# A delta-rule attention and two MLP layers in one kernel: layer 1 regrouped into six blocks of four chunks, with a longer opening chain

## The chip, the cores and the metric

The kernel runs on one core of a Trainium2 chip. TensorE (PE) multiplies matrices, VectorE (DVE), ScalarE (ACT) and GpSimd (POOL) work elementwise, SyncE (SP) issues the DMAs; each has its own instruction stream and waits for others by semaphores. The metric is the device time of one execution in microseconds (us); a change of under 0.5% can't be told from none here.

## The reference

```
attention, 4 batches x 8 heads x 768 steps, head size 48:
  k_n = k / (norm(k) + 1e-6);  state = 0
  per step t:  y[t]  = q[t] @ state
               state = state + beta[t] * outer(k_n[t], v[t] - k_n[t] @ state)
layer 1 (3072 tokens, 384 -> 2048 -> 384):
  h = x @ w_in
  g = h where h >= 1;  0 where h <= -1;  (h+1)^2/4 between
  x = g @ w_out
layer 2 (same sizes):  h = x @ w_in;  g = max(h, 0)^2;  out = g @ w_out
```

All data are float32. The kernel splits each operand of a layer into a rounded high part and a low remainder and sums three products (high x high, low x high, high x low).

## The kernel before

**Chunks, groups, blocks.** The 768 steps are 24 chunks of 32 steps, 128 tokens each (four batches). Attention works chunk by chunk: a gram of keys and queries (`gram`, L293), and a triangular inversion per group of chunks (`tri`: DVE transposes, a chain of small multiply-adds in `step`, on DVE for group 0, on POOL for the others). A chunk's chain is then `ks` (keys times state, L484), `tr` (inverse times values, L498), `qs` and `pu` (the two parts of y, tile yy, L484 and L518), `ku` (state update, tile sps, L530) and `xt` (transposes of y, L559). Each of these is 32 float32 matmuls of 32 rows, which the trace shows as 64 (two passes). `GROUPS` and `SIZES` say how many chunks make an inversion group and a layer-1 block.

**The opening** (all before `SL = 2 * NF`) is written out by hand: group 0 is two chunks, whose inverse is made of two halves on DVE and joined by small products (`joined`: ld writes z, L449; dld writes w, L457). Four more grams, for group 1, are made there too. The state update of these two chunks (`ku`) stands later, beside units 2 and 3.

**Units.** A unit is one of 16 slices of a layer's 2048 columns for one block: nine matmuls into h (L574, `hidden`), the activation on ACT and DVE, and nine matmuls into acc (`out1`) two units later. Layer 1's matmuls are as wide as the block, 256 or 384 columns; layer 2 uses 512. `exa` and `exb` hang the later chunks' steps, inversions and loads on half-unit slots; PE's order is as written, the others' is set by a scheduler after the opening.

**Weights.** Layer 1's 32 tiles come as 64-bit words (L160, at most two loads under way) and are joined, tile by tile, by two ACT passes (L178, L181), one DVE pass (L187), then split by ACT (L198) and DVE (L202), 128x384 each. Layer 2's go through DRAM and are placed during the last block.

Of the kernel before, what the change touches and what calls it, by code (L numbers as in the profile page):

```python
# [19 lines left out]
SIZES = [2, 2, 3, 3, 3, 3, 3, 2, 3]  # L20

GROUPS = [2, 4, 4, 4, 4, 4, 2]
# [3 lines left out]
def kernel(  # L26
# [39 lines left out]
    EAGER = 18  # L66
    AHEAD = 8
    RG = 3
    RAW = 3
    KQ, KG = 4, 2  # L70
    WT, WL = 3, 4
    GB = 2
    MANY = 4
    HEAD = 19
# [14 lines left out]
    pairs = {}  # L89

    def weight(i, f):

        if (i, f) not in pairs:
            t = wp.tile([P, 2, DM], F32R, tag=f"w{i}{f}", name=f"w{i}{f}")
            pairs[i, f] = t[:, 0], t[:, 1]
        return pairs[i, f]
# [4 lines left out]
    early = ["att0", "acc0", "att1", "acc1", "acc2"]  # L101
# [16 lines left out]

    def load_kq(c):
        if c < NCH:  # L120
            kqt[c] = fetch_kq(c, "kqt", KQ)

# [3 lines left out]
    def load_kg(c):  # L126
        if c < NCH and c not in kqg:
            kqg[c] = fetch_kq(c, "kqg", KG)

    def fetch_kq(c, tag, bufs):  # L130
        t = ring.tile([P, B2, H, 2 * T], F32, tag=tag, bufs=bufs, name="kqt")
        for o in range(2):
            nc.sync.dma_start(
                t[64 * o:64 * o + D].rearrange("p b h x -> p (b h x)"), kq[c, D * o:D * (o + 1)]
            )
        return t

    def load_kv(c):
        if c >= NCH:
            return  # L140
        t = kvt[c] = ring.tile([P, 2, H, D], F32, tag="kv", bufs=3, name="kv")
        nc.sync.dma_start(t.rearrange("p x h d -> p (x h d)"), kv[c])

# [5 lines left out]

    def load_w(x, key):
        w, f, i = key
        pool, tag, bufs = ring, "raw", RAW
        if w == 0:
            pool, tag, bufs = wp, f"w{i}{f}", 1
        raw = raws[key] = pool.tile([P, DM, 2], I32, tag=tag, bufs=bufs, name="raw")
# [11 lines left out]


    def convert_stages(key, box):
        def s0():
            raw = raws.pop(key)
            t = box["w"] = tmp("wt", WT)
            b = box["t"] = tmp("wl", WL)
            nc.scalar.activation(  # L178
                t, raw[:, :, 1].bitcast(F32), AF.Prelu, scale=2.0 ** -112, alpha=2.0 ** 32
            )  # L180
            nc.scalar.activation(  # L181
                b.bitcast(I32), raw[:, :, 0].bitcast(U32), AF.Copy, scale=7.49 * 2.0 ** -32
            )

        def s1():
            t, bits = box["w"].bitcast(I32), box["t"].bitcast(I32)
            nc.vector.scalar_tensor_tensor(  # L187
                bits, t, 3, bits, ALU.logical_shift_left, ALU.bitwise_or
            )

        return [s0, s1]


    def part_stages(key, box):
        _, f, i = key

        def s3():
            nc.scalar.copy(weight(i, f)[0], box["t"])  # L198

        def s4():  # L200
            hi, lo = weight(i, f)
            nc.vector.tensor_sub(lo, box["t"], hi.bitcast(F32))  # L202

        return convert_stages(key, box) + [s3, s4]
# [3 lines left out]
    def weight_items(w):  # L208

        keys = [(w, f, i) for f in range(NF) for i in range(2)]  # L210
        if w == 0:
            keys.sort(key=lambda k: (k[1] + LAG * k[2], -k[2]))

        def item(x):
            _, f, i = keys[x]
            box = {}
            if w == 0:
                r = part_stages(keys[x], box)
            else:
                r = convert_stages(keys[x], box)  # L220
                r.append(lambda: nc.sync.dma_start(w2f[f, :, i], box["t"]))
            s1 = r[1]
            r[1] = lambda: (s1(), ahead(x + 1 + (RAW if w else AHEAD)))
            return r

# [3 lines left out]
        def ahead(end):  # L229
            while todo and todo[0][0] < end:  # L230
                load_w(*todo.pop(0))
# [5 lines left out]
    def fetch_w2(f):  # L237
        w2r[f] = ring.tile([P, 2, DM], F32, tag="raw", bufs=RAW, name="w2r")
# [27 lines left out]
    def value(c):  # L266

        g, j = group_of[c]
        nc.gpsimd.tensor_mul(
# [10 lines left out]
    def gram(c, lo=0, hi=2, late=0, eng=None, side=0):  # L280
# [8 lines left out]
        src = kqt[c] if c < KQ else kqg[c]  # L289
# [9 lines left out]
        if c >= KQ:  # L299
            kqg.pop(c)  # L300
            if late < 2:
                load_kg(c + KG)
# [19 lines left out]
    HEADS = SIZES[0]  # L322
    cross = {}

    spare = {
        name: f"w{i}{NF - f}" for name, i, f in
        (("u0", 1, 1), ("u1", 1, 2), ("cross", 0, 1), ("z", 1, 3), ("l", 0, 2), ("d", 1, 4))
    }

    def cross_gram(a, c):  # L330
        x = cross[a, c] = wp.tile([P, H, 2, T], F32, tag=spare["cross"], name="cross")
# [14 lines left out]
    def tri(n, eng, halves=False):  # L346
        x = tx
        gm = ring.tile([P, T, T], F32, tag="gm", bufs=1, name="gm")
# [36 lines left out]
        def row():  # L385
            if halves:
                d = two(gm, both, both)
                eng.tensor_mul(
# [6 lines left out]
        def row2():  # L395
            if halves:
                eng.tensor_mul(
# [10 lines left out]
        def step(j):  # L408
# [15 lines left out]
            eng.tensor_add(rest, rest, t)  # L424
# [11 lines left out]
    def joined(n):  # L436
        l, z = (wp.tile([P, 2, H, T], F32, tag=spare[k], name=k) for k in "lz")
        d = wp.tile([P, GC * H, T2], F32, tag=spare["d"], name="d")
# [30 lines left out]
    def chunk_steps(c):  # L469
        n, j = block_of[c]  # L470
        g, gj = group_of[c]
        t = {}

# [22 lines left out]
        def tr():  # L496
# [7 lines left out]
            else:  # L504
                us[c] = wp.tile([P, H, D], F32, tag=spare[f"u{c}"], name="u")
            nc.scalar.copy(us[c], o)

        def qs():
            o = t["o"] = att([P, H, D], "yy", 1)
            of_state(o, 1)  # L510
            if c >= HEADS:
                kqt.pop(c)
                load_kq(c + KQ)

        def pu():
            o = t["o"]
            y = t["y"] = t["r"]
# [7 lines left out]
        def ku():  # L525
            k_ = kvt[c]
            if c < NCH - 1:
# [6 lines left out]
                if c >= HEADS:  # L534
                    pu()
# [5 lines left out]
            if c >= HEADS:  # L541
                nc.scalar.copy(t["y"], t["o"])
            done()

        def done():

            t["n"] = t.get("n", 0) + 1
            if t["n"] == 2:
                del kvt[c]
                load_kv(c + 3)  # L550

        def xt():
            if j == 0:
# [11 lines left out]
        return [ks, tr, qs, pu, ku, xt] if c < HEADS else [lambda: (ks(), qs()), tr, ku, xt]  # L565
# [18 lines left out]
    def hidden(layer, n, f):  # L584
# [18 lines left out]
        if layer == 0:  # L603
# [3 lines left out]
            marks[1] = nc.vector.tensor_scalar(g, r, 2.0, 0.5, ALU.min, ALU.mult)  # L607
            nc.scalar.activation(g, g, AF.Square)  # L608
            nc.vector.scalar_tensor_tensor(g, r, -1.0, g, ALU.add, ALU.max)  # L609
        else:  # L610
# [3 lines left out]
        def rest():  # L614
# [6 lines left out]
            nc.scalar.copy(ghi, g)  # L621
            nc.vector.tensor_sub(glo, g, ghi.bitcast(F32))  # L622
            gs[layer, n, f] = (ghi, glo)
# [8 lines left out]
    def out1(n, f):  # L632
# [10 lines left out]
        if f == NF - 1:  # L643
            for m, o in enumerate(acc.pop(n)):
                evac(m, o, x2[:, m, P * FIRST[n]:P * FIRST[n] + w], "wl", WL)
# [38 lines left out]
    def split_x2(n):  # L684
        def s0():
            homes = (("kqt", KQ), ("kqt", KQ), ("kqg", KG))
            both = [ring.tile([P, 2, N], F32R, tag=t, bufs=b, name="x2s") for t, b in homes]
            xh[n], xl[n] = ([x[:, i] for x in both] for i in range(2))
            for kt, x in enumerate(xh[n]):
# [8 lines left out]
    def flow(items, lag=1):  # L698

        steps = []  # L700
        for x, it in enumerate(items):
            for i, st_ in enumerate(it):
                while len(steps) <= x * lag + i:
                    steps.append([])
                steps[x * lag + i].append(st_)
        return [lambda fs=fs: [f() for f in fs] for fs in steps]

# [7 lines left out]
    first1, w1s = weight_items(0)  # L715
    first2, w2s = weight_items(1)
    w1f = flow(w1s)
    w1f.reverse()

    SPREAD = 3  # L720
    behind = [nullcontext]

    def more_w1(m=1):
        with behind[0]():
            for _ in range(m):
                if w1f:
                    w1f.pop()()

    with tc.manual_schedule():
        for c in range(GROUPS[0]):  # L730
            load_kq(c)
        nc.sync.dma_start(bet, beta)
        for c in range(GROUPS[0], KQ):
            load_kq(c)
        for c in range(KG):
            load_kg(KQ + c)
        for c in range(HEADS):
            load_kv(c)
        first1(EAGER)
        nc.gpsimd.memset(zero, 0.0)  # L740
        nc.gpsimd.memset(one, 1.0)
        nc.gpsimd.memset(tiny, 1e-36)
        nc.scalar.activation(st[:, 0, 0, 0:1], one, AF.Sqrt, bias=zero)
        nc.gpsimd.memset(mask, 1.0)
        nc.gpsimd.memset(tx, 0.0)
        for b in range(B):
            for o, op in enumerate((ALU.is_ge, ALU.is_gt)):
                m_ = mask[T * b:T * (b + 1), o]
                nc.gpsimd.affine_select(
# [5 lines left out]
        for c in range(GROUPS[0]):  # L755
            gram(c, 0, 1)
        begin, pre, steps, end = tri(0, V, True)
        begin()
        go(pre)
        for c in range(HEADS):  # L760
            save0(c)
        go([gram(c, late=2, eng=G) for c in range(GFIRST[1], GFIRST[2])])
        cross_gram(0, 1)
        masks = [gram(c, 1, 2, late=2, eng=G) for c in range(HEADS)]
        go(steps)
        for c in range(HEADS):
            value(c)
        go(masks)
        end()
        rows0()  # L770
        begin, pre, steps, end1 = tri(1, G)
        begin()
        ins = go(pre[:-2])
        behind[0] = lambda: tc.issue_after(ins.ins)
    ENGINES = {mybir.EngineType.PE}
    with tc.manual_schedule(engines=ENGINES):
        for f in (ld0, dld0):
            for c in range(HEADS):
                f(c)
        go(pre[-2:])  # L780
        go(steps)
        chains = [chunk_steps(c) for c in range(HEADS)]
        (k0, t0, q0, p0, _, x0), (k1, t1_, q1, p1, _, x1) = chains
# [176 lines left out]
```

## Time and profile before

| | |
|---|---|
| three runs, median (lowest to highest) | 1024.24 us (1022.86 to 1027.52) |
| the profiled execution | 1026.46 us, span of its instructions 1024.7 us |
| PE busy | 968.4 us, 95% of the span |
| DVE, ACT, POOL busy | 574.5, 465.2, 319.4 us |
| DMA | 80.83 MB, mean 79 GB/s |

A timeline row has start, length, engine, source line, operation, tiles written and read, shape, count, and in brackets the idle time of the engine before it with what ended that. "issue" as the ender means that the engine waited for nothing that the profile shows.

### The profile page before, as it was taken

Reading aid. Unit: us, or ns where it says so; the run is one execution under the profiler, and the core shown is the slowest. Engines: PE = TensorE matmul, PEld = TensorE weight load, DVE = VectorE, ACT = ScalarE, POOL = GpSimd, SP = SyncE. Lnnn points to the kernel's source line nnn. Section 1 sums busy time; section 2 is a strip of 40 time slices with the busy share of each in tenths; the row PEclk is TensorE's granted clock in tenths of the full one; section 3 lists DMA queues with packets and bytes.
Section 4 is the critical chain, followed back from the end, with each engine's and each line's share of the span. In section 5 each row is a group of like instructions: output and inputs, shape, how many; then the busy total and the mean of one; then the engine's idle time right before and its main releaser. Section 6 shows DMA issues by size and latency. Waiting matters only on the chain.

```text
span 1024.7 us, 32087 instructions
## 1 busy us (share of the span) xinstructions
PE 968.4 (95%) x14152; PEld 902.6 (88%) x14152; DVE 574.5 (56%) x994; ACT 465.2 (45%) x935; POOL 319.4 (31%) x476
## 2 busy tenths in 40 slices
PE   5357899999999999999999999999999999999998
PEld 4347898999999999999999999989989999899997
DVE  6988565775666677677465676543343333333333
ACT  2776465554555545555445554333333333333332
POOL 3792780492077049368022121120020200200000
PEclk9999999999999999999999999999999999999999
DMA  9774154442532534312023223010010000000000
GB/s 265 222 215 142 49 152 133 129 142 61 174 101 80 157 88 133 111 39 96 3 71 90 67 79 95 6 55 8 1 62 1 1 32 1 31 1 1 31 1 31
DMA packets 35244, 80.83 MB, mean 79 GB/s; under 512 B 4512, under 2 KB 15264, under 8 KB 35104
## 3 DMA queue, kind: packets, MB, share of 16 engines
q1 hardware_dynamic: 35104, 78.78, 25.9%
q8 instruction: 111, 1.82, 0.8%
q14 instruction: 29, 0.24, 0.1%
HBM read 63.03 MB, written 15.73 MB: 77 GB/s over the span
## 4 chain that ended last, share of the span: by engine, by line
PE 87%; DMA 6%; DVE 3%; ACT 2%; issue 1%; SPq 0%; ACTq 0%; DVEq 0%
PE acc L574 39%; PE h L574 38%; DMA raw<-in_w_dram 5%; PE yy L518 2%; PE sps L530 2%; PE tr L498 2%; PE ks L484 2%; PE g L293 1%; PE yy L484 1%; PE xt L559 1%; DMA kqt<-in_kq_dram 1%; DVE wl L187 0%; DVE g L609 0%; DVE w L202 0%; DVE gp L427 0%
## 5 line engine op out<-in xcount | busy, mean ns | idle before, releaser
L574 PE MATMUL acc<-w,gg 128*128 128x384 f32 x1152 | 218.4, 337 | 2.1 <-ACT e L629 2.1
L574 PEld LDWEIGHTS acc<-w,gg 128*128 128x128 f32 x1152 | 204.5, 187 | 10.7 <-ACT e L629 3.0
L574 PE MATMUL h<-x2s,w 128*128 128x512 f32 x864 | 213.8, 392 | 0.0
L574 PEld LDWEIGHTS h<-x2s,w 128*128 128x128 f32 x864 | 160.9, 188 | 28.3
L574 PE MATMUL h<-xh,w 128*128 128x384 f32 (+1 forms) x864 | 164.6, 327 | 3.5 <-ACT r L606 2.8
L574 PE MATMUL acc<-gh,w 128*128 128x384 f32 (+1 forms) x864 | 163.7, 325 | 1.6 <-ACT gh L621 1.6
L612 DVE TENSOR_TENSOR rg<-rg 128x512 f32<-128x512 f32 x96 | 71.3, 743 | 141.4 <-ACT rg L611 141.4
L574 PEld LDWEIGHTS h<-xh,w 128*128 128x128 f32 x864 | 139.6, 193 | 6.7 <-ACT r L606 3.7
L574 PEld LDWEIGHTS acc<-gh,w 128*128 128x128 f32 x864 | 136.7, 189 | 5.2 <-ACT gh L621 1.7
L611 ACT ACTIVATE rg<-h,zero 128x512 f32<-128x512 f32 x96 | 66.0, 687 | 137.4 <-PE h L574 137.4
L622 DVE TENSOR_TENSOR gg<-rg,gg 128x512 fp32r<-128x512 f32 x96 | 66.7, 695 | 104.5 <-ACT gg L621 104.5
L622 DVE TENSOR_TENSOR gl<-g,gh 128x384 fp32r<-128x384 f32 (+1 forms) x144 | 88.0, 611 | 64.5 <-ACT gh L621 60.3
L423 POOL TENSOR_TENSOR t<-tx,gm 128x30 f32<-128x30 f32 (+9 forms) x180 | 110.0, 611 | 19.3 <-DVE tx L402 5.9
L621 ACT CAST gh<-g 128x384 fp32r<-128x384 f32 (+1 forms) x144 | 68.7, 477 | 102.7 <-DVE g L609 78.4
L606 ACT ACTIVATE r<-h,one 128x384 f32<-128x384 f32 (+1 forms) x144 | 78.3, 543 | 81.5 <-PE h L574 80.3
L424 POOL TENSOR_TENSOR tx<-tx,t 128x30 f32<-128x30 f32 (+9 forms) x180 | 110.6, 615 | 14.0
L621 ACT CAST gg<-rg 128x512 fp32r<-128x512 f32 x96 | 59.7, 622 | 119.7 <-PE acc L574 112.7
L609 DVE SCALAR_TENSOR_TENSOR g<-r,g 128x384 f32<-128x384 f32 (+1 forms) x144 | 88.5, 614 | 39.9 <-ACT g L608 37.4
L607 DVE TENSOR_SCALAR g<-r 128x384 f32<-128x384 f32 (+1 forms) x144 | 62.4, 434 | 68.1 <-ACT r L606 67.1
L608 ACT ACTIVATE g<-g 128x384 f32<-128x384 f32 (+1 forms) x144 | 70.2, 487 | 54.5 <-DVE g L607 53.7
L574 PE MATMUL acc<-gl,w 128*128 128x384 f32 (+1 forms) x432 | 90.8, 318 | 1.9 <-DVE gl L622 1.9
L574 PE MATMUL h<-xl,w 128*128 128x384 f32 (+1 forms) x432 | 91.8, 322 | 0.0
(99 smaller groups left out, 923.9 us busy)
## 6 DMA issues: line engine op xcount, KB each, us to landing
raw<-in_w_dram SPq DMA_DIRECT2D x64, 384.0 KB, 3.8
kqt<-in_kq_dram SPq DMA_DIRECT2D x88, 192.0 KB, 4.1
kv<-in_kv_dram SPq DMA_DIRECT2D x24, 384.0 KB, 3.6
w2f<-wl SPq DMA_DIRECT2D x32, 192.0 KB, 3.1
w2r<-w2f SPq DMA_DIRECT2D x16, 384.0 KB, 3.0
x2r<-x SPq DMA_DIRECT2D x6, 768.0 KB, 4.8
out_dram<-e SPq DMA_DIRECT2D x23, 192.0 KB, 2.0
x<-e SPq DMA_DIRECT2D x18, 192.0 KB, 2.1
```

What stands on the lines that cost most here:

```text
L423: eng.tensor_mul(t, by.to_broadcast(shape), of.to_broadcast(shape))
L424: eng.tensor_add(rest, rest, t)
L484: per_bh(lambda b, h, p, pd: nc.tensor.matmul(o[p, h], kqt[c][pd, b // 2, h, x * T:(x + 1) * T], st[pd, b // 2, h], start=h == 0, stop=x = ...
L574: nc.tensor.matmul(o, *((r, l) if swap else (l, r)), **flags)
L606: marks[0] = nc.scalar.activation(r, h, AF.Relu, bias=one)
L607: marks[1] = nc.vector.tensor_scalar(g, r, 2.0, 0.5, ALU.min, ALU.mult)
L608: nc.scalar.activation(g, g, AF.Square)
L609: nc.vector.scalar_tensor_tensor(g, r, -1.0, g, ALU.add, ALU.max)
L611: marks[0] = nc.scalar.activation(r, h, AF.Relu, bias=zero)
L612: marks[1] = nc.vector.tensor_mul(g, r, r)
L621: nc.scalar.copy(ghi, g)
L622: nc.vector.tensor_sub(glo, g, ghi.bitcast(F32))
```

## The change

`SIZES` and `GROUPS` become six fours: every layer-1 block is one inversion group of four chunks, 512 columns wide. The opening now carries four chunks instead of two, and its order is given step by step; the full chain of the four chunks, state updates too, stands before the first unit. Grams of the first four chunks make both halves at once (`gram_of_head`), and POOL waits with its first multiplication until group 0's inversion has ended. Layer-1 weights are joined and split two tiles a pass (128x768, in place), four pairs in the opening, the rest one pair a unit inside the first twelve units (`between`). Scratch tiles share the space of the last three pairs, whose six loads come after the opening.

```diff
-SIZES = [2, 2, 3, 3, 3, 3, 3, 2, 3]
-GROUPS = [2, 4, 4, 4, 4, 4, 2]
+SIZES = [4] * 6
+GROUPS = [4] * 6
...
+    def sign_bits(raw):
+        low, high = raw[..., 0], raw[..., 1].bitcast(F32)
+        return (
+            lambda: nc.scalar.activation(high, high, AF.Prelu, scale=2.0 ** -112, alpha=2.0 ** 32),
+            lambda: nc.scalar.activation(
+                low, low.bitcast(U32), AF.Copy, scale=7.49 * 2.0 ** -32),
+        )
...
+    def upper(x):
+        nc.scalar.copy(weights(x)[:, :, 0], words[x])
+
+    def lower(x):
+        t = weights(x)
+        nc.vector.tensor_sub(t[:, :, 1], words.pop(x), t[:, :, 0].bitcast(F32))
...
+    def gram_of_head(c):
...
+        per_bh(lambda b, h, p, pd: nc.tensor.matmul(
+            g[p, h].rearrange("p x i -> p (x i)"),
+            kqt[c][pd, b // 2, h, 0:T], kqt[c][pd, b // 2, h],
+            start=h == 0, stop=True, skip_group_check=True,
+        ))
...
+    def between(f):
+        a = READY + f if READY + f < NP else None
+
+        def part(x):
+            if x == 0:
+                if a is not None:
+                    make(a)
+                some(1)
+            elif x == 1:
+                if a is not None:
+                    upper(a)
+            elif x == 2:
+                some(1)
+            elif a is not None:
+                lower(a)
...
-        chains = [chunk_steps(c) for c in range(HEADS)]
-        (k0, t0, q0, p0, _, x0), (k1, t1_, q1, p1, _, x1) = chains
-        for m, fs in enumerate([[k0, t0], [k1], [q0, p0], [t1_], [q1], [x0], [p1], [x1]]):
-            go(fs)
-            if m < 4:
-                more_w1(5)
...
+        whole_bits(2)
+        q1()
+        t2()
+        go(pre1[-2:])
+        steps1[0]()
+        go(steps1[1:])
+        whole_bits(3)
+        q2()
+        make(2)
+        k2()
+        p2()
+        upper(2)
+        y2()
+        lower(2)
+        s3()
+        dld0(3)
...
+        for x in range(NF):
+            unit(x, between(x))
```

On PE, between the last gram of the opening and the first unit, there stood in the kernel before (a group of 32 instructions a chunk and step; h is the first unit):

```order
L449 MATMUL z<-d,l 32x16 x64
L457 MATMUL w<-gp,z 32x16 x64
L498 MATMUL tr<-kv,gp 32x48 x32
L478 MATMUL ks<-u,cross 32x48 x32
L518 MATMUL yy<-u,gp 32x48 x32
L498 MATMUL tr<-kv,gp 32x48 x32
L478 MATMUL yy<-u,cross 32x48 x32
L559 MATMUL xt<-ident,kv 128x128 x3
L518 MATMUL yy<-u,gp 32x48 x32
L559 MATMUL xt<-ident,kv 128x128 x3
L574 MATMUL h<-xh,w_839 128x256 x6
```

The same stretch begins, in the changed kernel, as follows (L495, L503, L545, L525 and L531, L568 are its lines for z, w, tr, the two forms of ks and yy, and pu; 64 instructions into sps stand where the dots are):

```order
L495 MATMUL z<-room 32x16 x64
L503 MATMUL w<-gp,room 32x16 x64
L545 MATMUL tr<-kv,gp 32x48 x32
L495 MATMUL z<-room 32x16 x32
L525 MATMUL ks<-room 32x48 x32
L495 MATMUL z<-room 32x16 x32
L545 MATMUL tr<-kv,gp 32x48 x32
...
L503 MATMUL w<-gp,room 32x16 x32
L531 MATMUL ks<-st,kqt 32x48 x32
L525 MATMUL yy<-room 32x48 x32
L545 MATMUL tr<-kv,gp 32x48 x32
L531 MATMUL yy<-st,kqt 32x48 x32
```

The stretch has grown from 10 groups of 32 instructions to 26: z 4, w 4, tr 4, ks 3, yy 7 and sps 4. Nine groups of grams stand ahead of it in both.

On DVE, beside the units of the first block, there stood (wl and w are weights, g and gl the activation):

```order
L607 TENSOR_SCALAR g<-r 128x256
L202 TENSOR_TENSOR w_1252<-wl,w_1252 128x384
L202 TENSOR_TENSOR w_1262<-wl,w_1262 128x384
L187 SCALAR_TENSOR_TENSOR wl<-wt,wl 128x384
L202 TENSOR_TENSOR w_1364<-wl,w_1364 128x384
L609 SCALAR_TENSOR_TENSOR g<-r,g 128x256
```

and there stands now, once a unit:

```order
L660 TENSOR_SCALAR g<-r 128x512
L192 SCALAR_TENSOR_TENSOR wl<-raw 128x768
L663 SCALAR_TENSOR_TENSOR g<-r,g 128x512
L678 TENSOR_TENSOR gl<-g,gh 128x512
L226 TENSOR_TENSOR w_1658<-wl,w_1658 128x2x384
```

The weights, which a scheduler had laid in wherever DVE was free, now stand at fixed places between the steps of the activation, two instructions a unit.

## Rows read from the trace of the kernel before

**Rows 1.** The page's counts: PE, the instruction queue (packets, MB, share), weight loads.
```profile
PE 968.4 (95%) x14152; PEld 902.6 (88%) x14152; DVE 574.5 (56%) x994; ACT 465.2 (45%) x935; POOL 319.4 (31%) x476
...
q8 instruction: 111, 1.82, 0.8%
...
raw<-in_w_dram SPq DMA_DIRECT2D x64, 384.0 KB, 3.8
```

**Rows 2.** Busy time by stretch: its us, each engine, granted clock, DMA share, GB/s.
```profile
51.20:76.90 25.70, 14.42 (x353) 12.76 (x353) 21.81 (x29) 20.43 (x47) 23.27 (x31) 1.00 0.74 216
...
260.00:400.00 140.00, 140.00 (x2998) 132.45 (x2989) 93.58 (x167) 73.37 (x154) 66.36 (x105) 1.00 0.40 116
```

**Rows 3.** Timeline of PE in the opening.
```profile
28.30 1.54 PE L293 MATMUL g<-kqt 48*32 48x32 f32 x97 [2.67 <-issue]
29.77 0.61 PE L449 MATMUL z<-d,l 32*32 32x16 f32 x30
33.55 1.51 PE L449 MATMUL z<-d,l 32*32 32x16 f32 x98 [3.17 <-issue]
...
38.10 1.52 PE L457 MATMUL w<-gp,z 32*32 32x16 f32 x98 [2.65 <-issue]
...
43.26 1.00 PE L498 MATMUL tr<-kv,gp 32*32 32x48 f32 x34 [2.92 <-issue]
46.15 1.50 PE L478 MATMUL ks<-u,cross 32*32 32x48 f32 x64 [1.89 <-ACT u L506]
...
60.51 1.50 PE L518 MATMUL yy<-u,gp 32*32 32x48 f32 x64 [4.48 <-ACT u L506]
66.12 0.90 PE L559 MATMUL xt<-ident,kv 128*128 128x128 f32 x3 [4.11 <-ACT kv L523]
67.59 1.65 PE L574 MATMUL h<-xh,w 128*128 128x256 f32 x6 [0.57 <-ACT xh L561]
```

**Rows 4.** Timeline of PE: units of 256, 384 and 512 columns, two grams.
```profile
145.89 0.84 PE L574 MATMUL h<-xh,w 128*128 128x256 f32 x6
...
146.91 0.84 PE L574 MATMUL acc<-gh,w 128*128 128x256 f32 x6
...
163.94 1.99 PE L293 MATMUL g<-kqt 48*32 48x64 f32 x128
...
308.51 1.20 PE L574 MATMUL h<-xh,w 128*128 128x384 f32 x6
...
310.07 1.20 PE L574 MATMUL acc<-gh,w 128*128 128x384 f32 x6
...
705.39 2.21 PE L574 MATMUL h<-x2s,w 128*128 128x512 f32 x9
707.44 2.26 PE L574 MATMUL acc<-w,gg 128*128 128x384 f32 x12
```

**Rows 5.** Timeline of PE: one chunk's chain among 384-wide units.
```profile
301.21 0.88 PE L484 MATMUL ks<-st,kqt 48*32 48x48 f32 x64
...
302.70 1.32 PE L574 MATMUL acc<-gh,w 128*128 128x384 f32 x6
...
306.04 0.88 PE L498 MATMUL tr<-kv,gp 32*32 32x48 f32 x64
...
311.73 0.93 PE L530 MATMUL sps<-kv 32*48 32x48 f32 x64
...
313.40 1.31 PE L574 MATMUL h<-xh,w 128*128 128x384 f32 x6
```

**Rows 6.** Timeline of DVE: one weight pass, at two times.
```profile
36.97 0.55 DVE L202 TENSOR_TENSOR w<-wl,w 128x384 fp32r<-128x384 f32 x1
...
69.37 0.95 DVE L202 TENSOR_TENSOR w<-wl,w 128x384 fp32r<-128x384 f32 x1
```

**Rows 7.** Timeline of POOL: first and last instruction of group 1's inversion.
```profile
33.40 1.27 POOL L393 TENSOR_TENSOR gm<-gm,st 128x256 f32<-128x256 f32 x1 [0.19 <-DVE st L382]
...
82.17 0.27 POOL L424 TENSOR_TENSOR tx<-tx,t 128x30 f32<-128x30 f32 x1
```

More of the change, by code (lines that the diff above doesn't have):

```diff
@@ L185, in s1 @@
+            for f in sign_bits(raw):
+                f()
         def s1():
[L186 to L189, printed above, removed]
+            box["t"] = joined_words(box.pop("raw"), [P, DM])
         return [s0, s1]
[L194 to L204, printed above, removed]
+    words = {}
@@ L533, in ku @@
                 ))
-                if c >= HEADS:
+                if not apart:
                     pu()
@@ L582, with hidden @@
     marks = [None, None, None]
-    def hidden(layer, n, f):
+    def hidden(layer, n, f, between=lambda x: None):
         w = P * SIZES[n] if layer == 0 else N
@@ L714 @@
     V, G = nc.vector, nc.gpsimd
[L715 to L718, printed above, removed]
+    first2, w2s = weight_items()
+    SL = 2 * NF
     SPREAD = 3
[L721 to L727, printed above, removed]
+    NW, NP = 2 * NF, NF
+    EARLY, READY, HELD = 5, 4, 6
+    exa, exb = {}, {}
+    bits = [f for x in range(EARLY, NP) for f in (lambda x=x: halves(x)[0](), lambda x=x: halves(x)[1]())]
@@ new lines, with some @@
+    bits.reverse()
+    def some(m):
+        for _ in range(m):
+            if bits:
+                bits.pop()()
+    def between(f):
[12 more added lines that the diff above has]
+                lower(a)
+        return part
@@ new lines, with out_, unit, after @@
+    blocks = [(0, n) for n in range(NB)] + [(1, n) for n in range(NM)]
+    total = NF * len(blocks)
+    def out_(x):
+        g, f = divmod(x, NF)
+        (out1, out2)[blocks[g][0]](blocks[g][1], f)
+    def unit(x, between=lambda x: None):
+        g, f = divmod(x, NF)
+        rest = hidden(*blocks[g], f, between)
+        run(exa, 2 * x)
+        rest()
+        run(exb, 2 * x)
+        if x >= LAG:
+            out_(x - LAG)
+        run(exa, 2 * x + 1)
+        run(exb, 2 * x + 1)
+    def after(ins, first):
+        tc.add_manual_dep(
+            ins.ins, first.ins.name,
+            mybir.DependencyInfo(mybir.DependencyClass.Sync, mybir.DependencyReason.DATA),
+            reason="GpSimd keeps still beside the inversion",
+        )
@@ new lines @@
+        pre[0]()
+        go(pre[1:])
+        cross_gram(0, 1)
+        masks = [gram(c, late=2, eng=G) for c in (4, 5)]
+        for c in range(FIRST_GROUP):
+            save0(c)
+        whole_bits(0)
+        whole_bits(1)
+        masks += [gram(c, late=2, eng=G) for c in (6, 7)]
+        ins = go(steps)
+        rows0()
+        end()
+        after(value(0), ins)
+        value(1)
+        mask_of_head(0)
+        mask_of_head(1)
+        go(masks)
+        value(2)
+        value(3)
+        mask_of_head(2)
@@ new lines @@
+        mask_of_head(3)
+        begin1, pre1, steps1, end1 = tri(1, G)
+        (s0, t0, q0, p0, k0, x0, _), (s1, t1, q1, p1, k1, x1, _), \
+            (s2, t2, q2, p2, k2, x2_, y2), (s3, t3, q3, p3, k3, x3, y3) = [
+                chunk_steps(c) for c in range(FIRST_GROUP)]
+        ld0(0)
+        ld0(1)
+        make(0)
+        dld0(0)
+        dld0(1)
+        upper(0)
+        s0()
+        t0()
+        lower(0)
+        ld0(2)
+        make(1)
+        s1()
+        upper(1)
+        ld0(3)
@@ new lines @@
+        t1()
+        begin1()
+        k0()
+        lower(1)
+        pre1[0]()
+        k1()
+        dld0(2)
+        go(pre1[1:-2])
+        s2()
+        whole_bits(2)
[14 more added lines that the diff above has]
+        dld0(3)
+        make(3)
+        t3()
+        halves(4)[0]()
+        p1()
@@ new lines, with steps_of @@
+        x2_()
+        upper(3)
+        q3()
+        p3()
+        y3()
+        lower(3)
+        x1()
+        halves(4)[1]()
+        q0()
+        p0()
+        x3()
+        x0()
+        k3()
+        for x in range(NW - HELD, NW):
+            load_w(needed[x])
+        turn[0] = None
+        put(0, 12, end1)
+        put(0, 11, lambda: value(4))
+        put(0, 12, lambda: value(5))
+        put(0, 14, lambda: value(6))
+        put(0, 21, lambda: value(7))
+        for c, at_ in ((4, (12, 13, 15, 16)), (5, (17, 18, 20, 21)),
+                       (6, (22, 23, 24, 25)), (7, (26, 27, 29, 30))):
+            def steps_of(c=c, box={}):
+                if c not in box:
+                    box[c] = chunk_steps(c)
+                return box[c]
+            for i, slot in enumerate(at_):
+                put_a(0, slot, lambda i=i, g=steps_of: g()[i]())
```

360 lines of the change are left out of this document (177 added, 183 removed).

## The prediction

> **What bounds the kernel now.** I read the busy time by stretch first, then PE's timeline in the opening and among the units, then DVE and POOL in the opening. From 260 to 400 us PE is busy for all of 140.00 us; from 51.2 to 76.9 it is busy for 14.42 of 25.70 [rows 2]. So the kernel is an opening, in which PE mostly stands, and then a stretch in which PE is the bound: the end is the start of the first unit plus the PE work that is left. The first unit starts at 67.59 [rows 3]; 957.1 us of the 1024.7 us span follow it.
>
> The reader is to see in [rows 3] that PE stands at regular places, for 2.67, 3.17, 2.65 and 2.92 us, with "issue" behind each: no engine and no data transfer is waited for. From one restart to the next there are 128 matmuls (97 and 30 with one record lost, then 98 and 30 twice), and each has a weight load, so 256 instructions. The page counts 2 x 14152 PE records and 111 packets on the instruction queue with 1.82 MB: 255 records and 16.4 KB a packet [rows 1]. So PE's program comes in pieces of 256 instructions, and in this stretch each piece is waited for. Between the restarts at 28.30 and 43.26 lie three pieces, 4.99 us each; the work in the first is 2.08 us (28.30 to the end of the row at 29.77). After 43.26 no such stand is seen in the opening, and there PE waits for ACT for 1.89, 4.48 and 4.11 us anyway: a piece can come during a wait for something else. Among the units it costs little: a piece full of long matmuls lasts longer than its fetch.
>
> [...]
>
> **The change part by part.**
>
> *The opening on PE.* Nine groups of grams come first in both; four of them grow from 32 to 64 columns. [...] That is 0 to 3.8 us, partly beside the inversion on DVE; I take 1.9. So z starts at 29.8 + 1.9 = 31.7.
>
> From z to the first unit stand 26 groups where there were 10. A group is 64 matmuls as the trace counts them, so two make a piece: 13 pieces. The order puts other PE work between a step and the step that needs it, so waits for ACT and DVE are mostly over when PE gets there, and then nothing covers a fetch. At 4.99 us a piece that is 64.9 us. Four transposes come to it, about 0.6 each without the row's tail (0.90 at 66.12 [rows 3]): 2.4. First unit: 31.7 + 64.9 + 2.4 = 99.0, later by 31.4. Bounds: with every fetch hidden, 13 x 2.08 = 27.0 instead of 64.9 and the start at 61.1, or 71.6 with the three ACT waits (10.5 us) left in; with the longest stand seen, 3.17, a piece is 5.25 and the start 102.4.
>
> *What leaves the stretch after it.* Two whole chains: 1.49 (ks and yy, 301.21 to 302.70), 0.88 (tr), 1.67 (sps and pu, 311.73 to 313.40) [rows 5] and under 0.45 of transposes (half of 0.90) are 4.5, twice 9.0. Two grams, 2.0. The state updates of the first two chunks, 0.93 each [rows 5]: 1.9. Together -12.9.
>
> *Six wide blocks.* A unit has 18 matmuls of the block's width. Start to start, nine take 1.02 us at 256 columns, 1.56 at 384 and 2.05 at 512 [rows 4]. Before: 3 blocks x 16 units x 2.04 + 6 x 16 x 3.12 = 397.4. After: 6 x 16 x 4.10 = 393.6. The cost goes with the columns, and those are the same; nothing is won by fewer instructions where PE is full. acc at 512 columns isn't shown; twelve matmuls of 384, the same 4608 columns as nine of 512, last 2.26 us with their tail, and with that as the upper bound a unit takes 4.31 and the layer 413.8. I take the h row nearest to it and 1.8 more for the changes of tile: -2, between -4 and +16.
>
> *Weights two tiles a pass.* In the opening, ACT and DVE have less to do than before (four pairs, not most of the tiles), beside a PE that stands: nothing. Inside the first twelve units each adds two 768-wide passes on DVE and three on ACT. A 384-wide DVE pass takes 0.55 us at 36.97, where POOL is still, and 0.95 at 69.37, where POOL inverts [rows 6]; scaled by width, a unit's three 512-wide and two 768-wide passes are an estimated 4.4 or 7.6 us, against 4.1 on PE alone. POOL's inversion of group 1 lasts from 33.40 to 82.44, 49 us [rows 7]. Its preparation now stands behind the thirteenth of the 26 groups, at 31.7 + 6.5 x 4.99 = 64, so it ends at about 113: 14 us of the first units lie beside it. DVE does 14 / 7.6 = 1.8 units there and PE could do 3.4, less what its own slow first microseconds cost. I take +5, between 0 and +20.
>
> *Loads.* With two under way and 3.8 us from issue to landing [rows 1], a tile comes every 1.9 us; 26 are queued ahead of the chain, 49 us, and the chunks' loads between them stand in front of nothing that PE needs before 99. The six that were held back are for units 13 to 15. Nothing, while the chain is as long as forecast; if it were 30 us shorter, the first pairs would still be there in time, one pair a unit.
>
> *The rest.* One inversion fewer on POOL and DVE, three fewer block ends: beside a full PE, nothing.
>
> **Sum.** 1024.7 + 31.4 - 12.9 - 2 + 5 = 1046.2 in the span. The profiled execution took 1.8 us beyond its span and 2.2 more than the median, so 1046 against 1024.24.
>
> **The rivals.**
>
> *The fetch hides behind the chain's own waits, and the kernel gets faster.* The mechanism is that of 43.26 to 67.59: each step of one chunk waits for ACT or DVE, and the next piece comes meanwhile. For it: no "issue" stand there [rows 3]. Against it: those waits came from ACT and DVE queues full of weight passes, which are gone, and a wait that covers a fetch costs about as much as the fetch. First unit at 71.6: 1024.7 + 4.0 - 12.9 - 2 + 5 - 0.4 = 1018. It decides from a piece cost of about 3.0 us downward.
>
> *Half of it hides.* Each piece has one wait in its middle, and costs 3.5 us: 13 x 3.5 = 45.5, first unit at 79.6, 1026: no change.
>
> *Conversion becomes the bound of the first block.* The words are now read 8 bytes apart by DVE; if that halves its pace, or POOL's inversion reaches further into the block, twelve units take 7.6 us where PE with its share of attention takes about 5.5: 25 us instead of the 5 taken, 1066. Against it: the pass at 36.97 is short as soon as POOL rests.
>
> **How the numbers follow.** The forecast 0.67, with a range of its own from 1034 (a piece at 4.1 us) to 1058; half hidden 0.13; all hidden 0.13; conversion 0.07. Under 0.5% from the median (1019.1 to 1029.4) can't be told from no change. Faster: most of the hidden case, 0.10. Same: the half-hidden case and the edge of the hidden one, 0.16. Slower: 0.74. A range of 1018 to 1062 leaves out about half of the hidden case and most of the last.
>
> **What would show it.** In the changed kernel's PE timeline: the first 512-wide h near 99; ahead of it ten or more "issue" rows of 2.5 to 3.2 us, 128 matmuls apart, and few waits for ACT or DVE; from unit 4 on a full PE; h at 2.05 us per nine; DVE passes of 768 at about 1.1 us, or 1.9 beside POOL, and POOL's inversion ending near 113. It is wrong if the first unit starts before 85, or if PE stands for more than 20 us within the first block.

## The result, and the profile after

The changed kernel takes 1036.21 us (median of five, 1035.11 to 1040.43) against 1024.24; the ratio is 1.0117, with a 95% interval from 1.0085 to 1.0149. That is slower, as forecast, by 12 us and not by 22. The profiled execution is the slowest of the five: 1040.43 us, span 1038.6, against 1026.46 and 1024.7 before.

PE's timeline in the opening, to set beside [rows 3]:

```profile
32.95 0.61 PE L495 MATMUL z<-room 32*32 32x16 f32 x29 [0.34 <-DVE room L491]
34.02 1.52 PE L495 MATMUL z<-room 32*32 32x16 f32 x98 [0.46 <-issue]
...
38.02 1.52 PE L503 MATMUL w<-gp,room 32*32 32x16 f32 x99 [2.10 <-issue]
...
57.47 1.04 PE L580 MATMUL sps<-u,kv 32*48 32x48 f32 x36 [2.40 <-issue]
...
69.66 1.04 PE L580 MATMUL sps<-kv 32*48 32x48 f32 x37 [0.48 <-issue]
...
79.74 0.94 PE L545 MATMUL tr<-kv,gp 32*32 32x48 f32 x35 [3.11 <-issue]
...
82.61 0.90 PE L612 MATMUL xt<-ident,kv 128*128 128x128 f32 x3 [0.58 <-ACT kv L573]
...
90.12 1.65 PE L627 MATMUL h<-xh,w 128*128 128x512 f32 x6
...
92.30 1.54 PE L627 MATMUL h<-xh,w 128*128 128x512 f32 x6
...
94.36 1.54 PE L627 MATMUL h<-xh,w 128*128 128x512 f32 x6
```

z starts at 32.95 (29.77 before), the first unit at 90.12 (67.59 before, 99.0 forecast). Between lie eleven stands that end with "issue", 0.46 to 3.11 us; waits for ACT and DVE are nearly gone, the longest 0.58. From 34.02 to 79.74 PE restarts ten times more, one piece of its program each: 4.57 us a piece. That these stands are fetches can be seen in the same trace, on the queue that carries the instructions (105 packets of 16 KB): each of the eleven ends 1.2 to 1.5 us after such a packet has landed, and the packet itself took 0.9 to 1.5 us. In all thirteen profiles it is the same for the 133 stands of this kind ahead of 112 us: 1.0 to 1.7 us behind a packet of 0.9 to 1.8 us.

```profile
q8 instruction: 105, 1.72, 0.7%
```

The same by stretch, the opening's chain and the rest (us; busy time of PE, PEld, DVE, ACT, POOL with counts; granted clock, DMA share, GB/s), of the kernel after and then of the one before:

```profile
32.95:90.12 57.17, 37.77 (x1676) 33.46 (x1676) 21.24 (x34) 15.79 (x30) 35.77 (x52) 1.00 0.66 189
90.12:1038.60 948.48, 923.92 (x11172) 782.05 (x11164) 479.18 (x723) 409.78 (x696) 257.72 (x342) 0.99 0.22 66
```

```profile
29.77:67.59 37.82, 14.62 (x652) 12.69 (x647) 32.80 (x53) 28.08 (x65) 31.97 (x46) 1.00 0.80 224
67.59:1024.70 957.11, 939.35 (x12930) 877.05 (x12930) 521.59 (x898) 428.42 (x852) 276.88 (x405) 1.00 0.23 68
```

The chain before the first unit grew from 37.82 to 57.17 us: PE works 23.2 us more in it and stands 3.8 us less. After the first unit PE has 15.4 us less to do (939.35 to 923.92) and stands 6.8 us longer (24.6, not 17.8). The waits there that are new or longer, in PE's timeline:

```profile
108.14 2.93 PE L627 MATMUL h<-xh,w 128*128 128x512 f32 x6 [3.78 <-ACT r L659]
...
133.55 0.88 PE L545 MATMUL tr<-kv,gp 32*32 32x48 f32 x64 [3.73 <-DVE gp L471]
...
150.53 0.89 PE L531 MATMUL yy<-st,kqt 48*32 48x48 f32 x64 [3.02 <-DVE xl L615]
...
308.19 1.77 PE L627 MATMUL acc<-gh,w 128*128 128x512 f32 x4 [2.86 <-ACT e L686]
```

The products behind such a wait run at the low pace for some microseconds: six of h take 2.93 at 108.14 and 1.54 at 92.30; the granted clock of 87.3 to 128 us reads 0.92. The fourth row is the longest of five waits at block ends, 7.1 us in all (2.1 before; 3.9 to 5.7 in six kernels below that leave the block ends alone). ACT's own row shows why its copy is late, with the buffer that it shares with layer 2's weights:

```profile
307.55 0.58 ACT L686 COPY e<-acc 128x512 f32<-128x512 f32 x1 [4.10 <-DMA w2f<-wl]
```

In DVE's timeline a 768-wide weight pass of the first units takes 1.10 to 1.34 us beside POOL's inversion, which ends at 106.8, 1.58 beside the multiplication of kv that POOL does next, and 0.95 behind that; the four passes beside the inversion in the opening, at 64.87 to 84.80, take 0.91 to 1.16:

```profile
99.18 1.25 DVE L192 SCALAR_TENSOR_TENSOR wl<-raw 128x768 int32<-128x768 int32 x1
...
106.76 3.85 POOL L285 TENSOR_TENSOR kv<-kv,nt 128x384 f32<-128x384 f32 x3
107.36 1.58 DVE L226 TENSOR_TENSOR w<-wl,w 128x768 fp32r<-128x768 f32 x1
...
114.70 0.95 DVE L192 SCALAR_TENSOR_TENSOR wl<-raw 128x768 int32<-128x768 int32 x1
```

### The profile page after: what moved, and what is told of

Its sections match the earlier page's. It is cut to its first block, busy times and chain, and to the rows that moved or that the text cites. A ratio compares the mean times of both kernels' runs of the same rounds, so it can differ in the third digit from the quotient of the medians.

```text
span 1038.6 us, 30010 instructions
## 1 busy us (share of the span) xinstructions
PE 979.5 (94%) x13416; PEld 831.2 (80%) x13416; DVE 515.3 (50%) x801; ACT 435.9 (42%) x745; POOL 298.8 (29%) x414
## 4 chain that ended last, share of the span: by engine, by line
PE 85%; DVE 6%; issue 3%; DMA 3%; ACT 2%; SPq 1%; POOL 0%; ACTq 0%; DVEq 0%; POOLq 0%
PE h L627 37%; PE acc L627 36%; PE sps L580 2%; PE tr L545 2%; PE yy L531 2%; PE yy L568 2%; PE ks L531 2%; DMA w2f<-wl 1%; DVE gp L471 1%; PE g L309 1%; DVE wl L192 1%; PE xt L612 1%; ACT r L659 1%; DMA room<-in_kq_dram 1%; DVE g L660 1%
## 5 line engine op out<-in xcount | busy, mean ns | idle before, releaser
L627 PE MATMUL acc<-gh,w 128*128 128x512 f32 x576 | 155.5, 404 | 6.5 <-ACT e L686 5.4
L627 PE MATMUL h<-xh,w 128*128 128x512 f32 x576 | 154.9, 405 | 3.8 <-ACT r L659 3.8
L659 ACT ACTIVATE r<-h,one 128x512 f32<-128x512 f32 x96 | 65.9, 687 | 115.2 <-PE h L627 114.4
L660 DVE TENSOR_SCALAR g<-r 128x512 f32<-128x512 f32 x96 | 48.2, 502 | 124.0 <-ACT r L659 123.6
L678 DVE TENSOR_TENSOR gl<-g,gh 128x512 fp32r<-128x512 f32 x96 | 73.4, 764 | 61.2 <-ACT gh L676 45.0
L468 POOL TENSOR_TENSOR tx<-tx,t 128x30 f32<-128x30 f32 (+9 forms) x150 | 99.4, 663 | 11.7
L676 ACT CAST gh<-g 128x512 fp32r<-128x512 f32 x96 | 59.6, 621 | 80.2 <-DVE g L663 56.0
L663 DVE SCALAR_TENSOR_TENSOR g<-r,g 128x512 f32<-128x512 f32 x96 | 74.9, 781 | 22.2 <-ACT g L662 21.9
L627 PE MATMUL h<-xl,w 128*128 128x512 f32 x288 | 83.3, 398 | 0.1
L627 PE MATMUL acc<-gl,w 128*128 128x512 f32 x288 | 82.2, 394 | 0.0
L662 ACT ACTIVATE g<-g 128x512 f32<-128x512 f32 x96 | 60.5, 630 | 34.6 <-DVE g L660 33.0
```

The costliest lines, as they stand in the source:

```text
L468: return eng.tensor_add(rest, rest, t)
L627: nc.tensor.matmul(o, *((r, l) if swap else (l, r)), **flags)
L659: marks[0] = nc.scalar.activation(r, h, AF.Relu, bias=one)
```

## The experiments

Ratios are to runs of the kernel before on the same chip; the changed kernel's own is 1.0117. "First h" is the start of the first 512-wide unit in the profile, 90.12 in the changed kernel.

**What does a piece cost: fewer, more, and narrow ones.** Three kernels change only how many y groups stand in the opening; no step of the state waits for them.

`no_y` leaves out the seven yy groups; one 128x384 product a chunk writes yy in their place, so y of these four chunks is only u:

```diff
-            of_state(o, 1)
+            if not apart:
+                of_state(o, 1)
...
+            if apart:
+                nc.tensor.matmul(
+                    o.rearrange("p h d -> p (h d)"), ident, us[c].rearrange("p h d -> p (h d)"),
+                    start=True, stop=True)
```

> The changed kernel, but the seven yy groups of the opening (queries times state, queries times u, for the first four chunks) are left out; one 128x384 product per chunk writes yy instead, so y of these chunks is only u. 448 of the matmuls as the trace counts them go, 896 instructions with their weight loads, some 3.4 pieces of 256. Theory (PE's program comes in pieces, about 4.57 us each: ten from the restart at 34.02 to that at 79.74): the first 512-wide h comes 3.4 x 4.57 = 15.5 us earlier, at about 75, down to 80 if new waits for ACT and DVE turn up between the steps that now stand close together. Rival one (PE's own work at its low pace: 1.29 us a yy group, start to start at 62.41 and 63.70): 9.0 us earlier, 81. Rival two (the chain of ACT and DVE steps sets the start, the yy groups only fill its waits): no change, 90. Time: 1036 less the same.

`more_q`, six groups more:

```diff
-            of_state(o, 1)
+            for _ in range(3 if apart else 1):
+                of_state(o, 1)
```

> The changed kernel with the queries-times-state groups of chunks 1 to 3 issued three times over: six groups more in the opening, 384 matmuls, 768 instructions, three pieces, with nothing new to wait for; the result stays. Theory (pieces): first h 3 x 4.57 = 13.7 us later, at 104, with three more stands in the opening. Rival one (PE's own work): 6 x 1.29 = 7.7 later, 98. Rival two (the chain): the groups go into its waits, which are 1.4 us in all, so under 7.7 later. Time: 1036 plus the same.

`narrow_q`, twelve groups of 16 columns more:

```diff
+            for _ in range(4 if apart else 0):
+                narrow(o)
             of_state(o, 1)
```

> The changed kernel with twelve more groups in the opening, each like queries times state of chunks 1 to 3 but only 16 of 48 columns wide: 768 matmuls, 1536 instructions, six pieces, of little work; the result stays. The three wide pieces of the run before cost 3.1 us each, about what they work, so the question is open again. Theory (pieces have a cadence of their own: restarts in that run stood 3.45 to 4.28 us apart however little was done between): 6 x 3.5 to 4.3 = 21 to 26 us more, first h at 111 to 116, and a stand of 1.5 to 2.5 us in every piece. Rival (only PE's own work counts, and stands come from elsewhere): a 16-column group takes 64 x 13.4 ns = 0.86 (98 matmuls in 1.31 us from 33.55 to 34.86 of the kernel before), so 10.3 us more, first h at 100.

Measured ratios: no_y 1.003 (1.0011 to 1.0049), more_q 1.0174 (1.0144 to 1.0204), narrow_q 1.0318 (1.0296 to 1.0341). The stretch from the first z to the first h in each (columns as above), no_y, more_q, narrow_q:

```profile
30.20:76.33 46.13, 29.58 (x1236) 24.36 (x1236) 21.69 (x34) 15.85 (x30) 25.66 (x36) 1.00 0.77 217
```

```profile
31.01:98.06 67.05, 47.02 (x2061) 41.97 (x2061) 21.49 (x34) 15.99 (x30) 43.46 (x65) 1.00 0.58 162
```

```profile
31.90:109.95 78.05, 50.52 (x2444) 45.22 (x2445) 21.14 (x34) 15.85 (x30) 45.99 (x73) 1.00 0.50 137
```

Against 57.17 us that is 11.0 less for 3.4 pieces, 9.9 more for 3, 20.9 more for 6: 3.2, 3.3 and 3.5 us a piece. One execution differs from another by about 1 us here: end1_early and w2_later below, which have the changed kernel's opening, take 56.9 and 55.9. The runs' ratios give 8.9 less, 5.8 more and 20.6 more, each give or take 4, so the price of the first two, 2.6 and 1.9 us a piece by the ratios, is known less well than that of the third, 3.4. The chain as the bound (no change) is out at once. The first two alone don't tell pieces from work: PE's busy time went by 8.2 and 9.3 us with them, close to the whole difference, and my 4.57 a piece missed both (15.5 and 13.7 expected). narrow_q tells them apart: its groups add 12.8 us of busy time, 10.3 by the rival's reckoning, and cost 20.9. The reader sees it in its timeline, where rows of 128 matmuls take 1.9 us and the next restart comes 3.5 to 4.5 us after the last:

```profile
64.98 1.91 PE L524 MATMUL yy<-room 32*32 32x16 f32 x128 [1.88 <-issue]
...
69.53 0.66 PE L524 MATMUL yy<-room 32*32 32x16 f32 x34 [2.65 <-issue]
...
77.19 1.90 PE L529 MATMUL yy<-st,kqt 48*32 48x16 f32 x128 [1.05 <-issue]
...
80.92 0.67 PE L529 MATMUL yy<-st,kqt 48*32 48x16 f32 x35 [1.83 <-issue]
```

So, by the profiles of these three, an extra piece costs about the larger of its work and some 3.5 us.

**Does work hide the fetch?** `long_fill` adds long products of few instructions:

```diff
+        if turn[0] is not None and name in ("z", "w", "tr", "ks", "yy"):
+            for _ in range(2):
+                nc.tensor.matmul(
+                    t.rearrange("p a b -> p (a b)")[:, 0:P], ident, ident, start=True, stop=True)
```

> The changed kernel with two 128x128 float32 products of the identity ahead of the z, w, tr, ks and yy groups of the opening (38 in all, 152 instructions, their output is overwritten): long work in few instructions. By the single 128x384 product of the run without y (1.65 us with its tail at the low pace, 0.81 at the full one) one of them takes some 0.5 or 0.25 us, 19 or 9 in all. Theory (a piece's fetch is what PE stands for, and runs beside PE's work): the added work falls into the 18 us of stands, first h between 85 and 97. If the pace rises with it from 1.29 to 0.88 us a group, the cadence of the pieces still holds it above 82. Rival one (PE's own work and its pace set the opening): at the full pace 26 x 0.41 - 9 = 2 us earlier and more as stands go with it, first h 75 to 88; at the low pace 19 us later, 109.

Measured: 1.0123 (1.0101 to 1.0145), first h at 90.29, no change. From the first added product to the first h PE is busy 14 us longer than in the changed kernel's chain, and stands 7.7 us, not 19.4:

```profile
30.79:90.29 59.50, 51.83 (x1756) 44.81 (x1753) 20.38 (x34) 16.18 (x30) 33.35 (x50) 0.66 0.64 181
...
60.52 0.30 PE L508 MATMUL w<-gp,room 32*32 32x16 f32 x12 [2.46 <-issue]
...
67.11 1.50 PE L550 MATMUL tr<-kv,gp 32*32 32x48 f32 x64
...
79.59 0.88 PE L550 MATMUL tr<-kv,gp 32*32 32x48 f32 x64
```

The longest stand left is 2.46. Of the 14 us added, 11.7 fell into the stands, so PE's own work doesn't make them. A gain from a higher pace hardly came: a tr group at 67.11 still takes 1.50 us with its tail, as yy at 60.51 in [rows 3], and only from about 78 us on is the pace the higher one. The granted clock of the stretch reads 0.66 here and 1.00 in the changed kernel, but that isn't the products' doing: in end1_early below, whose opening is the changed kernel's with the same 1.50 us a group, it reads 0.53. In the opening this reading does not follow the pace:

```profile
32.69:89.60 56.91, 37.81 (x1680) 33.44 (x1677) 19.93 (x34) 16.07 (x30) 33.82 (x48) 0.53 0.68 190
```

**The waits after the first unit.** Three kernels move one thing each. Their gains are near the scatter: the part behind the first unit is 943.0, 941.7 and 941.0 us in their profiles, and 942.4 to 946.9 in the four kernels above, which leave it alone (948.5 in the changed kernel's, its slowest execution). What is clear in each is which wait goes.

`inv_early` issues group 1's inversion before chunk 1's ks:

```diff
         make(1)
+        begin1()
+        pre1[0]()
+        go(pre1[1:])
+        go(steps1)
         s1()
```

> The changed kernel with group 1's preparation and its inversion on POOL issued ahead of chunk 1's ks, so that POOL starts at about 47 and not at 61.56 and ends about 14 us earlier, near 93, when the units have just begun. Theory (in the first four units DVE, slowed beside POOL, is the bound: its 768-wide passes take 1.18 to 1.58 us there and 0.95 after POOL has ended): the waits of 1.04 and 3.78 us before the fourth and fifth unit's products go, and the half pace after them (2.8 us): 5 to 7 us less. Rival (the order of ACT's queue or the number of h buffers sets these waits): less than 2 us of change. First h stays at 90, give or take 1.

Measured: 1.0078 (1.0053 to 1.0102), 4 us less than the changed kernel, with intervals that overlap. POOL's first step stands at 47.03 and its inversion ends at 84.6, before the units begin, so DVE's passes take 0.95 from 96.9 on. But the wait of 3.78 us hardly shrinks:

```profile
106.20 1.76 PE L627 MATMUL h<-xh,w 128*128 128x512 f32 x6 [3.25 <-ACT r L659]
```

DVE beside POOL was at most a small part of it; the rest is ACT's queue, where the passes of one unit (two of 0.9 us and one of 0.83 for weights, three for the activation) come round every 4.2 us, and PE, three h ahead, waits for a free one.

`end1_early` and `w2_later` change one number each:

```diff
-        put(0, 12, end1)
+        put(0, 9, end1)
```

> The changed kernel with the closing transposition of group 1 (2.0 us on DVE) three half-unit slots earlier, slot 9 and not 12. Theory (tr of chunk 4 waits 3.73 us at 133.55 only because this transposition stands late in DVE's queue): that wait goes, and the half pace of the h behind it (2.83 and 1.28 us where 1.54 and 0.85 are usual): 5 us less, 1031. Rival (DVE is full in these units, 1.15 us of a unit idle, so the wait comes back at an activation): less than 2 us of change.

Measured: 1.0064 (1.0031 to 1.0096), 5.4 us less; the row with 3.73 has no wait any more, and the wait for xl behind it stays (3.69).

```diff
-                    put(n, 1 + 3 * i, *later(*w2s.pop(0)))
+                    put(n, 4 + 3 * i, *later(*w2s.pop(0)))
```

> The changed kernel with one edit: layer 2's weight items stand three half-unit slots later in each block of layer 1, so that no transfer out of a wl tile is under way when a block's evacuation on ACT asks for one of the two wl tiles. Theory (the tag wl went from four tiles to two with the change, and that is what acc waits for at block ends: 7.1 us in five waits for ACT e, 2.9 the longest): the waits go, and with the half pace behind them 7 to 9 us, 1028 to 1030. Rival (ACT is busy there anyway, or the wait turns up at a weight item): under 3 us.

Measured: 1.0064 (1.0038 to 1.009), 5.4 us less; of the waits for ACT's e 1.4 us are left. The transfer out of the shared buffer is the cause, though the gain is smaller than expected (5.4 us, not 7 to 9); a kernel with four buffers again was not run.

**All of it, and more.** `after_eased` joins the three and takes ACT's weight passes out of the first three units; `after_eased2` finishes seven pairs in the opening, where DVE and ACT stand; `after_eased3` puts ACT's passes into gaps that no step of the chain follows, and two grams where PE waits for h. The last one's edit, in part:

```diff
-    EARLY, READY, HELD = 5, 4, 6
+    EARLY, READY, HELD = 8, 7, 6
...
-        a = READY + f if READY + f < NP else None
+        on = f not in (0, 1, 7, 8)
+        a = READY + sum(x not in (0, 1, 7, 8) for x in range(f))
...
-        for c, slot in ((8, 8), (10, 10)):
+        for c, slot in ((8, 6), (10, 8)):
```

> The changed kernel with four things put elsewhere at the same amount of work: group 1's inversion early and its closing transposition at slot 9 (as in the two runs before); the two ACT passes of pairs 5 to 7 in the opening, where ACT stands, and none in the first three units; layer 2's weight items three slots later in each block, so that a block's evacuation on ACT does not ask for a tile that a weight's transfer still reads. Theory: the waits after the first unit (20.6 us) go one by one: 5 for the inversion and its transposition each, 3.25 for ACT's r, 7.1 for ACT's e at block ends and the half pace behind it: 1036 - 4 - 5 - 4 - 6 = 1017, give or take 4. Rival (the waits move: PE is ahead of ACT and DVE in these blocks, which are the bound there): no better than the sum of the two runs before, 1027.

Measured: 0.9994 (0.9978 to 1.001): 12.6 us less than the changed kernel by the ratios, near the sum of the three (14.8) though a fourth thing was moved, and level with the kernel before. Joined, the three are clear of the scatter: 932.2 us behind the first unit.

> The eased form of the changed kernel, with seven pairs of weights (not four) finished in the opening, where DVE and ACT stand, the pairs' ACT passes ahead of the chain's steps that wait for PE, and no weight pass in units 0, 7 and 8. Theory (in these units DVE and ACT are the bound, and in the opening they are not since PE waits there for its program): first h stays at 87 to 90; the waits of 2.4 (ACT r), 1.0 (gh) and 3.7 us (DVE xl) and the half pace behind them go: 7 to 9 us less than the eased form, 1016, ratio 0.992. Rival (DVE passes now stand ahead of the chain's in the opening): first h 3 to 6 us later, no gain.

Measured: 0.9974 (0.9954 to 0.9994), 2 us less than `after_eased` and not 7 to 9. After the first unit the wait for xl shrinks from 3.7 to 1.9 us and that for gh goes, but the one for ACT's r stays (2.5), and the first h is 2.5 us later, at 89.83: a new wait stands in the opening, where ACT has weights ahead of a step of the chain, as the rival had it for DVE:

```profile
81.55 0.90 PE L612 MATMUL xt<-ident,kv 128*128 128x128 f32 x3 [4.47 <-ACT kv L573]
```

> The second eased form with three more moves: ACT's passes of pairs 5 to 7 into the gaps of its queue before the third chunk's tr, so that none stands between that chunk's tr and its y; the first two later grams one unit earlier, where PE waits for an h buffer; no weight pass in unit 1 either. Theory: the wait of 4.5 us for ACT (kv) in the opening goes and the first h comes at 85 to 86 instead of 89.83; the wait of 2.5 us for ACT's r is filled with the grams: together 5 to 7 us less than the second eased form, ratio 0.990 to 0.993 of the kernel before. Rival (the opening is held by PE's program, so a wait for ACT that goes comes back as a stand for the next piece): first h at 88 to 90 and at most 2 us less.

Measured: 0.9932 (0.9914 to 0.9949), 1018.72 us: the one version that beats both kernels by more than 0.5%. That is 4.3 us less than the second eased form, a little under the 5 to 7 expected. The profile doesn't show where they went: it caught the slowest of the six executions, and its span, 1019.2, is that of the second eased form's profile. The wait of 4.47 is down to 0.58, but the first h is at 91.64, since a stand of 5.67 us for a piece came into this execution; the rest is 1.8 us shorter:

```profile
49.22 0.93 PE L525 MATMUL ks<-room 32*32 32x48 f32 x34 [5.67 <-issue]
...
91.64:1019.20 927.56, 915.63 (x11171) 777.50 (x11164) 470.40 (x717) 401.97 (x687) 243.27 (x320) 1.00 0.23 67
```

**The kernel before, eased in the same way.** `before_eased` uses the merged grams and keeps weights out of the second chunk's chain:

```diff
-            gram(c, 0, 1)
+            gram_of_head(c)
...
-                more_w1(5)
+                more_w1(3)
```

> The kernel before with two things of its opening changed: the grams of chunks 0 and 1 made both halves at once (two groups, one piece, fewer, as the changed kernel does), and three not five steps of weights put after each of the first four links of the chain, so that none stands in ACT's queue within the second chunk's chain. Theory: one piece (4.0 to 5.0 us) and the waits of 4.48 and 4.11 us for ACT go; first unit at 67.59 - 4 - 7 = 56 to 58, time 1013 to 1016. Rival (weights then come late to the first block's units and the gain is given back): 1022 to 1026.

Measured: 1.0003 (0.9989 to 1.0017), no gain: the rival's time. The first unit does start at 56.38, 11 us earlier, but the part behind it takes 964.8 us where it took 957.1: PE waits there for ACT and DVE, whose queues are full of weight passes, and runs at the low pace (three acc take 1.01 us at 72.01 and 0.51 at 101.70):

```profile
64.71 1.93 PE L293 MATMUL g<-kqt 48*32 48x64 f32 x64 [3.81 <-ACT r L628]
...
72.01 1.01 PE L596 MATMUL acc<-gl,w 128*128 128x256 f32 x3 [2.29 <-DVE gl L644]
...
108.36 1.50 PE L520 MATMUL tr<-kv,gp 32*32 32x48 f32 x64 [3.40 <-DVE kv L516]
```

Before, ACT and DVE use the opening to convert weights; a shorter opening only moves that work beside the units.

## Why the prediction was right, and where it was off

*The direction and its cause held.* The longer chain in pieces of 256 instructions was to make the first unit later, by more than what leaves the stretch behind it. It is 22.5 us later, and the rest is 8.6 us shorter in the profiles. The stands at the restarts are fetches, as the packets of the instruction queue show: each ends 1.2 to 1.5 us behind one.

*The mis-sized term is the piece.* I took 13 pieces at 4.99 us, 2.08 of work and 2.9 of standing, from the stretch between 28.30 and 43.26. The chain has 37.77 us of work and 19.4 of stands: 2.9 and 1.5 a piece, if all 13 are counted and the transposes, 2.4 of the 57.17 us, are left in; without them a piece is 4.2. The stretch that I read consisted mostly of 16- and 32-column groups; groups of 48 columns work longer (1.29 us each, start to start), and what they work longer comes off the stand. The sum fell too: the five pieces to 57.47 average 4.69 us, the four behind them 3.98. Behind 79.74 PE stands for no piece any more: transposes and waits cover the fetch. So the signs named were half right: ten restarts 128 matmuls apart and few other waits, but stands of 0.46 to 3.11, only two of them over 2.5. From z to the first unit it was 57.2 us where I had 67.3; z came 1.3 us later than forecast, so the first unit is 8.9 us early. In the profiles the rest came out 1.3 us longer than forecast, and the span 7.6 us shorter; the median lies another 2 us lower, since the execution profiled after was 4.2 us above its median, not 2.2.

How much of a fetch shows is bounded by narrow_q and long_fill: at 1.9 to 2.6 us of work a piece it shows as 1.0 to 2.7 us, and with long products between the groups most of it is hidden (stands of 7.7 us in all, not 19.4). The rival in which all of it hides (1018) was out. The rival in which half hides had the price of an extra piece (3.5 us), but the whole chain averages 4.2.

*What leaves the stretch, and the width,* were -12.9 and -2: PE's work behind the first unit is less by 15.4. Nine h take 2.06 us start to start (2.05 forecast); nine acc of 512 columns take 2.18 (from 121.63 to 123.81 in the rows below), against 1.66 at 384 (from 310.07 in [rows 4] to 311.73 in [rows 5]), in proportion to the columns again.

```profile
121.63 1.66 PE L627 MATMUL acc<-gh,w 128*128 128x512 f32 x6
123.13 0.85 PE L627 MATMUL acc<-gl,w 128*128 128x512 f32 x3
123.81 1.54 PE L627 MATMUL h<-xh,w 128*128 128x512 f32 x6
```

*Weights two a pass,* +5: PE stands 6.8 us more behind the first unit. POOL's inversion ended at 106.8 (113 forecast), and DVE's passes take 0.95 alone and 1.10 to 1.34 beside it (1.1 and 1.9 forecast); why they are slower beside it no run here shows. That the size came near is luck. With POOL's inversion out of the way (inv_early) the longest wait of the first units goes only from 3.78 to 3.25 us, and ACT's queue is the bound there; and I had not seen two waits whose removal took some 5 us each off the time, by the ratios (5.4 each, give or take 4 to 5). One is the closing transposition at slot 12. The other is at block ends: I put three ends fewer at nothing, and did not follow the tag wl from four buffers to two and to ACT's copy, which shares it. With these waits the sign "from unit 4 on a full PE" failed as well: PE waits 3 us and more at 108.14, 133.55 and 150.53.

*Loads,* nothing: no wait for a weight's load stands on PE behind the first unit. Ahead of z, where I had none either, the grams wait 2.77 and 0.56 us for loads of kqt in this execution.

*The grams,* +1.9: no run shows this term, an estimate of mine. In the opening of the changed kernel's profile the two groups of 64 columns at 28.92 take 3.69 us with their tail, 1.8 each, where 97 matmuls of 32 columns took 1.47 (28.30 to 29.77 in [rows 3]), 0.97 for a group of 64 matmuls. z came 3.2 us later; in the other profiles whose windows are shown above it starts between 30.20 and 32.69, so 1.9 is within what one execution differs from another.

What stays open is why some packets start late. In the traces a piece is three times: from a restart to the start of the next packet 1.0 to 5.3 us, the packet 0.9 to 1.8, and from its end to the next restart 1.0 to 1.7. The first makes the long pieces: it is 3.2 of the 5.92 us that end at 57.47, 3.7 of the 6.35 that end at 79.74, and 5.3 in the piece with the stand of 5.67.

It goes with the other DMA traffic. Of the pieces of 128 matmuls between two such stands, over all profiles, nine have a DMA share of up to 0.24: there the first time is 1.0 to 1.2 us, and they last 3.46 to 3.88, whether PE works 1.9 or 3.25 of them. That is the floor of some 3.5. The 29 with a share over 0.8 last 3.9 to 8.1. Two pieces of narrow_q with the same work, and one of the changed kernel:

```profile
64.98:69.53 4.55, 1.91 (x128) 1.80 (x128) 0.03 (x1) 0.00 (x0) 3.77 (x11) 1.00 0.73 205
77.19:80.92 3.73, 1.90 (x129) 1.80 (x129) 0.00 (x0) 0.00 (x0) 3.27 (x6) 1.00 0.02 4
```

```profile
51.55:57.47 5.92, 3.52 (x128) 3.24 (x129) 0.38 (x1) 0.73 (x2) 0.00 (x0) 1.00 0.94 263
```

The 4.99 of the forecast was read at shares of 0.79 to 1.00, so its size may be the loads' doing. No run moved the loads alone, and DMA traffic alone doesn't say it: the 6.35 us end with a stand of 3.11 in which the share is 0.10.

## What to carry to other kernels

Count PE's instructions, not only its microseconds: where small matmuls stand back to back, 256 instructions last at least some 3.5 us here, and 38 long products between them cost nothing (long_fill). When a change removes buffers of a shared tag, follow every user of the tag, those at block ends too. A shorter opening gains only what ACT and DVE did not need it for.

## What was not expected of the hardware

- A piece's cost is near a floor of 3.2 to 3.5 us at the margin in the profiles, whether the pieces are added or taken away, and not the 4.99 of a few stands in a row. The next packet of instructions starts 1.0 us or more after PE's restart, so in the opening it is not fetched far ahead.
- The granted clock that the profile gives for the opening reads 1.00, 0.66 or 0.53 (changed kernel, long_fill, end1_early), while groups of 48 columns take the same 1.50 us with their tail at 62 to 67 us in all three, and 0.88 among the units.
- Behind a wait of 3 to 4 us among units PE runs at the low pace for some microseconds: nine h then take 4.14, 3.75 and 3.84 us from start to start (at 108.14, 134.36 and 151.34) where 2.06 is usual, so these waits cost 1.7 to 2.1 us more than the 3.0 to 3.8 that they show.
